# A gated mixer of linear attention and a spatial MLP: b_sp by a small TensorE transpose, folds over two chunks, the first tile by column half, attention drifting ahead, the last output in two banks

## The chip, the cores and the metric

The kernel runs on one core of one Trainium2 chip. Times are device microseconds (us) of a whole execution. "Span" is the time from the first to the last instruction of the one execution that the profiler took; the execution's own time is about 2 us longer (229.2 and 231.05 us for the profiled run of the kernel before). In this kernel TensorE does the matmuls, ScalarE the activation functions (gelu, exp, scaled copies), VectorE elementwise work and reductions, GpSimd small odds and ends; SP only issues DMAs. "Bank" stands here for the PSUM buffer that one matmul group writes.

## The reference, cut to what matters

```python
# x: 2048 x 512, bf16; H = 32 heads of 16; F = 1376, Fh = 688
g = sigmoid((x * gate_w).sum(-1, keepdims=True))
# A: linear attention, feature map softmax(+-q Wphi), softmax(+-k Wphi)
q, k, v = heads(x @ wqkv); pq = q @ w_phi; pk = k @ w_phi          # per head
phi = lambda p: concat(softmax(p), softmax(-p))
kv = phi(pk).T @ v; z = phi(pk).sum(0)
a = (phi(pq) @ kv) / (phi(pq) @ z + 1e-6) @ wo
# B: gated MLP with a product over the sequence
z1, z2 = split(gelu(x @ w_in)); z2 = layernorm(z2)
b = (z1 * (w_sp @ z2 + b_sp[:, None])) @ w_out                      # w_sp: 2048 x 2048
return g * a + (1 - g) * b
```

Of the kernel before, what the change touches and what calls it, by code (L numbers as in the profile page):

```python
# [8 lines left out]
ALU = mybir.AluOpType  # L9
# [25 lines left out]
def kernel(  # L35
# [21 lines left out]
    psF_cm = tc.tile_pool(name="psF", bufs=1, space=bass.MemoryType.PSUM, side="right")  # L57
# [20 lines left out]
    bT_bf = pers.tile([P, NT], BF16, name="bT_bf")  # L78
# [15 lines left out]
    gaterow = early.tile([NDT, P], BF16, name="gaterow")  # L94
    warm = early.tile([P, CH], BF16, name="warm")
# [20 lines left out]
    nc.gpsimd.dma_start(out=gaterow[:, :], in_=gate_w.rearrange("(dt p) -> dt p", p=P))  # L116
    nc.sync.dma_start(out=xs[:, 0, :], in_=x2[0:P, :])
# [12 lines left out]
    for q in range(2, NCH):  # L130
# [8 lines left out]
    )  # L139
    nc.sync.dma_start_transpose(  # L140
        out=bT_bf[:, :], in_=B_b_sp.rearrange("(t p) -> t p", p=P)
# [50 lines left out]
    def z_mm(tt, wt, w, mid=None):  # L192
        zp = psA.tile([P, 2, CH], FP32, name="zp")
        for dt in range(NDT):
            if dt == 2 and mid is not None:
                mid()
            lhsT = xT[:, dt, tt * P:(tt + 1) * P]
            for j in range(2):
                n = HF if j == 0 else w - HF
                nc.tensor.matmul(  # L200
                    zp[:, j, 0:n], lhsT=lhsT, rhs=wt[:, dt, j * HF:j * HF + n],
                    start=(dt == 0), stop=(dt == NDT - 1),
                )
        return zp

    def z2_tile(tt, mid=None):
        zp = z_mm(tt, w_z2, FH + 1, mid)
        z2v = z2all[:, tt, :].rearrange("p (j n) -> p j n", j=2)
        nc.scalar.activation(out=z2v, in_=zp[:, :, 0:HF], func=AF.Gelu_apprx_tanh)  # L209
        nc.vector.tensor_copy(out=glog[:, tt:tt + 1], in_=zp[:, 1, HF:HF + 1])  # L210
        for j in range(2):
            nc.vector.bn_stats(out=bn6[:, tt, j, :], in_=z2v[:, j, :])  # L212
        nc.vector.bn_aggr(out=mv[:, tt, :], in_=bn6[:, tt, :, :].rearrange("p j s -> p (j s)"))
# [26 lines left out]
    def x_T(i):  # L240
# [3 lines left out]
        nc.vector.tensor_copy(out=xT[:, :, i * P:(i + 1) * P], in_=tp[:, :, :])  # L244

    def gate_T():
        gt = psF.tile([P, NDT], BF16, name="gt", tag="pq", bufs=2)
        nc.tensor.transpose(gt[:, :], gaterow[:, :], ident[0:NDT, 0:NDT])
        for dt in range(NDT):
            nc.vector.tensor_copy(out=w_z2[:, dt, FH:FH + 1], in_=gt[:, dt:dt + 1])  # L250

# [28 lines left out]
    with tc.manual_schedule(engines={mybir.EngineType.PE}):  # L280
        warm_up(8)
        x_T(0)
        gate_T()
        for i in range(4):
            z2_tile(i, (lambda k=i + 1: x_T(k)) if i < 3 else None)
        for c in range(NCH):
            ts = list(range(c * 4, c * 4 + 4))
            last = c == NCH - 1
            for tt in ts:
                if c > 0:  # L290
                    z2_tile(tt)
                if last:
                    fold(1, tt % 4)
            for tt in ts:
                z1_tile(tt)
                if last:
                    fold(0, tt % 4)
            z2_norm(ts)
            if c == NCH - 2:
                wphi_fold()  # L300
# [10 lines left out]
    kvacc = [psM.tile([P, NG, 256], FP32, name=f"kvacc{a}", tag="kvat", bufs=2) for a in range(2)]  # L311

# [3 lines left out]
    def k_tile(tt):  # L316
# [4 lines left out]
        ek = work.tile([P, 2, D], BF16, name="ek", bufs=4)  # L321
# [11 lines left out]
    def v_tile(tt, rk):  # L333
# [4 lines left out]
        vr = work.tile([P, 2, NG, P + 8], BF16, name="vr", bufs=3)  # L338
# [59 lines left out]
    def attn_tile(tt):  # L398
# [33 lines left out]
        oT = work.tile([P, NG, P], BF16, name="oT", bufs=3)  # L432
# [8 lines left out]
    def ba_tile(tt, uT, oT):  # L441
        acc = mm_tile()
        for g in range(NG):
            nc.tensor.matmul(acc[:, :], lhsT=oT[:, g, :], rhs=wo_t[:, g, :], start=(g == 0), stop=False)  # L444
        for ft in range(NFT):
            nc.tensor.matmul(acc[:, :], lhsT=uT[:, ft, :], rhs=w_out_t[:, ft, :], start=False, stop=(ft == NFT - 1))  # L446
        ob = work.tile([P, D], BF16, name="ob")
        if tt < NT - 1:
            nc.scalar.activation(out=ob[:, :], in_=acc[:, :], func=AF.Copy, scale=g_inv[:, tt:tt + 1])  # L449
            nc.scalar.dma_start(out=out2[tt * P:(tt + 1) * P, :], in_=ob[:, :])  # L450
        else:
            hd = D // 2
            nc.scalar.activation(out=ob[:, 0:hd], in_=acc[:, 0:hd], func=AF.Copy, scale=g_inv[:, tt:tt + 1])
            nc.scalar.dma_start(out=out2[tt * P:(tt + 1) * P, 0:hd], in_=ob[:, 0:hd])
            nc.vector.tensor_scalar(
                out=ob[:, hd:D], in0=acc[:, hd:D], scalar1=g_inv[:, tt:tt + 1], scalar2=None, op0=ALU.mult)
            nc.sync.dma_start(out=out2[tt * P:(tt + 1) * P, hd:D], in_=ob[:, hd:D])

    nc.vector.tensor_copy(out=bT[:, :], in_=bT_bf[:, :])
    oTs = {}  # L460
    uTs = {}
    with tc.manual_schedule(engines={mybir.EngineType.PE}):
        ks = {0: k_tile(0)}
        pend = []
        for tt in range(NT):
# [5 lines left out]
            if len(pend) > 1:  # L471
# [3 lines left out]
        nc.vector.reciprocal(out=g_inv[:, :], in_=g_1p[:, :])  # L475
        gg_half(0, 0)
# [4 lines left out]
        gg_half(0, 1)  # L481
        uTs[0] = u_T(0)
        oTs[0] = attn_tile(0)
        for tt in range(1, NT):
            gg_half(tt, 0)
            if tt == NT - 1:
                oTs[tt] = attn_tile(tt)
            gg_half(tt, 1)
            uTs[tt] = u_T(tt)
            if tt < NT - 1:  # L490
                oTs[tt] = attn_tile(tt)
            if tt >= 2:
                ba_tile(tt - 2, uTs.pop(tt - 2), oTs.pop(tt - 2))
        for tt in (NT - 2, NT - 1):
            ba_tile(tt, uTs.pop(tt), oTs.pop(tt))
# [30 lines left out]
```

## The kernel before: the parts that the change and the argument touch

The kernel has three stages. Stage one computes z2 and z1 for 16 tiles of 128 rows in four chunks, and folds w_phi into the q and k weights. Stage two computes k, v and q tile by tile and sums kv. Stage three computes the spatial product in half tiles (`gg_half`), one attention tile beside each, and the output tile (`ba_tile`) two tiles later. A scheduler orders all engines' instructions except TensorE's, which stand in the order written.

```python
    # stage 0: loads. b_sp's transpose is a DMA, queued on SP behind x, w_in, wqkv
    ...
    nc.sync.dma_start_transpose(out=bT_bf[:, :], in_=B_b_sp.rearrange("(t p) -> t p", p=P))
    ...
    def z2_tile(tt, mid=None):
        zp = z_mm(tt, w_z2, FH + 1, mid)      # 4 slices dt x 2 column halves j; column 688 is the gate
        nc.scalar.activation(out=z2v, in_=zp[:, :, 0:HF], func=AF.Gelu_apprx_tanh)
        nc.vector.tensor_copy(out=glog[:, tt:tt + 1], in_=zp[:, 1, HF:HF + 1])   # gate logit
        ... # statistics for the layernorm
    ...
    with tc.manual_schedule(engines={mybir.EngineType.PE}):
        warm_up(8)                            # 8 matmuls of 512 columns on zeros
        x_T(0)                                # transposes of x tile 0, copied by VectorE
        gate_T()                              # gate_w into column 688 of w_z2
        for i in range(4):
            z2_tile(i, (lambda k=i + 1: x_T(k)) if i < 3 else None)
        for c in range(NCH):
            ts = list(range(c * 4, c * 4 + 4))
            last = c == NCH - 1
            for tt in ts:
                if c > 0: z2_tile(tt)
                if last: fold(1, tt % 4)      # k weights; copied by ScalarE or VectorE
            for tt in ts:
                z1_tile(tt)
                if last: fold(0, tt % 4)      # q weights
            z2_norm(ts)
            ...
    ...
    nc.vector.tensor_copy(out=bT[:, :], in_=bT_bf[:, :])     # written after stage one, needed in stage three
    with tc.manual_schedule(engines={mybir.EngineType.PE}):
        ... # k, v, q tiles, kv sums one tile late
        nc.scalar.activation(out=g_el[:, :], in_=glog[:, :], func=AF.Exp)
        ...
        for tt in range(1, NT):
            gg_half(tt, 0)
            if tt == NT - 1: oTs[tt] = attn_tile(tt)
            gg_half(tt, 1)
            uTs[tt] = u_T(tt)
            if tt < NT - 1: oTs[tt] = attn_tile(tt)
            if tt >= 2: ba_tile(tt - 2, uTs.pop(tt - 2), oTs.pop(tt - 2))
        for tt in (NT - 2, NT - 1): ba_tile(tt, uTs.pop(tt), oTs.pop(tt))
```

The softmax here doesn't subtract the row's maximum and nothing guards it: scores larger than these inputs give would overflow.

## Time and profile before

| | before |
|---|---|
| time, median of 3 runs | 230.83 us (229.98 to 231.57) |
| span of the profiled run | 229.2 us |
| TensorE busy | 212.7 us, 93% |
| first z1 matmul | 12.24 us |
| last z2 gelu begins | 48.22 us |
| first k matmul; first exp of k | 56.28 us; 57.54 us |
| first matmul of the spatial product | 105.32 us |

The landmarks in the lower half of the table are starts of instructions in the timeline. They cut the span into stretches.

From the page of the profile: busy time of the engines (share of the span, instructions), and TensorE's granted clock, in tenths, in 40 slices of the span.

```profile
PE 212.7 (93%) x1417; PEld 129.6 (57%) x1437; DVE 151.1 (66%) x382; ACT 76.3 (33%) x121; POOL 13.3 (6%) x50
...
PEclk9999799999999999999999999999999999999997
```

TensorE is nearly full, so what can be won are its holes. These lines are from the timeline: start, duration, engine, line of the kernel, operation, output<-inputs, and in brackets the idle time before it and what ended it. `w_z_66` is w_z2 and `w_z_65` is w_z1.

```profile
21.03 1.15 SPq L140 DMA_TRANSPOSE bT_bf<-in_B_b_sp_dram  x1
...
25.11 0.17 DVE L459 CAST bT<-bT_bf 128x16 f32<-128x16 bf16 x1 [7.60 <-DMA bT_bf<-in_B_b_sp_dram]
...
25.40 2.46 PE L200 MATMUL zp<-w_z_66,xT 128*128 128x344 bf16 x8 [4.82 <-DVE glog L210]
```

VectorE sat idle for 7.60 us in front of the bT cast, because b_sp's DMA had not landed. VectorE takes its instructions in order here (its next one starts at 25.20 us, when the cast is all but done), and the gate-logit copies that free the zp banks stood behind the cast; so TensorE sat idle for 4.82 us.

The view of stretches gives, for each stretch of time, its length and the busy time of the engines (TensorE's matmuls, its weight loads, VectorE, ScalarE, GpSimd, each with its number of instructions), the granted clock (1.00 is full), the DMA share and GB/s:

```profile
20.60:25.40 4.80, 0.00 (x0) 0.00 (x0) 0.29 (x3) 0.74 (x1) 0.00 (x0) 1.00 0.93 232
25.40:27.65 2.25, 2.25 (x8) 1.16 (x8) 2.18 (x9) 0.00 (x0) 0.00 (x0) 0.50 1.27 288
27.65:29.00 1.35, 1.35 (x7) 0.74 (x6) 1.29 (x5) 0.74 (x1) 0.00 (x0) 0.57 1.27 289
29.00:30.00 1.00, 1.00 (x9) 0.66 (x8) 0.88 (x3) 0.41 (x1) 0.00 (x0) 1.00 1.28 291
```

After the hole the clock is halved, to 0.50, for about 3.4 us: all of the second stretch, and 1.15 us of the third, whose mean is 0.57. Two more places are the last z chunk and the end. From the timeline, the last z chunk:

```profile
53.90 0.38 PE L269 MATMUL fps<-wphi,wqkT 128*128 128x128 bf16 x4 [1.55 <-DVE wq_p L278]
...
56.28 1.89 PE L319 MATMUL mm<-wk_p,xT 128*128 128x512 bf16 x7 [0.61 <-ACT z1all L217]
```

The end of the kernel before, from the same timeline:

```profile
222.43 1.04 PE L444 MATMUL mm<-wo_t,oT 128*128 128x512 bf16 x4 [1.43 <-DMA oT<-o]
...
224.80 0.47 ACT L453 ACTIVATE ob<-mm,g_inv 128x256 bf16<-128x256 f32 x1 [3.08 <-PE mm L446]
...
225.31 0.48 DVE L455 TENSOR_SCALAR ob<-mm,g_inv 128x256 bf16<-128x256 f32 x1 [6.91 <-ACT ob L453]
```

A fold waits 1.55 us for a VectorE copy, the first k tile 0.61 us for ScalarE, the last output tile 1.43 us for the transposed attention output oT; and VectorE's copy of the last half starts only when ScalarE's has ended.

### The profile page before, as it was taken

The numbers are of one execution on the slowest core, as the hardware profiler recorded it, in microseconds if no ns is written. First come the engines' busy times: TensorE is split into PE (matmuls) and PEld (weight loads), VectorE is DVE, ScalarE is ACT, GpSimd is POOL, SyncE is SP. The second block draws the span as 40 slices with busy tenths as digits, with TensorE's granted clock in tenths as the row PEclk, the third lists the DMA queues.
The fourth block names the chain that finished last, engine by engine and source line by source line (L and its number), as shares of the span: only waits on it lengthen the run. The fifth ranks groups of instructions, "written<-read, shape, count | busy, mean of one in ns | idle before, by whom it ended". The sixth has DMA issues, their size and how long they took to land.

```text
span 229.2 us, 3683 instructions
## 1 busy us (share of the span) xinstructions
PE 212.7 (93%) x1417; PEld 129.6 (57%) x1437; DVE 151.1 (66%) x382; ACT 76.3 (33%) x121; POOL 13.3 (6%) x50
## 2 busy tenths in 40 slices
PE   7895599996999999999999999999999999999972
PEld 2563366673455555556676666566666666566630
DVE  3650548585799999997887655765557655666810
ACT  2355156688867667663001101110011101110020
POOL 7020020110000000000000000000000000000000
PEclk9999799999999999999999999999999999999997
DMA  6999999999700000000143223323132223323140
GB/s 213 220 220 181 264 248 288 180 254 282 232 0 0 0 3 0 0 6 0 34 60 80 57 51 78 79 48 69 47 80 60 57 59 70 80 59 60 46 103 24
DMA packets 71395, 22.30 MB, mean 97 GB/s; under 512 B 65953, under 2 KB 71377, under 8 KB 71377
## 3 DMA queue, kind: packets, MB, share of 16 engines
q1 hardware_dynamic: 67952, 19.40, 41.3%
q10 hardware_dynamic: 3392, 2.66, 3.5%
q8 instruction: 11, 0.18, 0.3%
q14 instruction: 8, 0.06, 0.1%
q0 software_dynamic: 32, 0.00, 0.0%
HBM read 3.70 MB, written 2.10 MB: 25 GB/s over the span
## 4 chain that ended last, share of the span: by engine, by line
PE 75%; SPq 8%; DVE 7%; DMA 5%; ACT 2%; issue 2%; POOL 1%
PE mm L388 32%; PE zp L200 8%; PE mm L446 8%; PE mm L336 5%; PE mm L364 5%; PE mm L444 5%; PE mm L319 5%; SPq L134 3%; SPq L129 2%; DMA bT_bf<-in_B_b_sp_dram 2%; PE kvacc_683 L354 2%; PE kvacc_682 L354 2%; SPq L131 2%; DVE bn_84 L212 1%; DMA oT<-o 1%
## 5 line engine op out<-in xcount | busy, mean ns | idle before, releaser
L388 PE MATMUL mm<-z2all,wspT 128*128 128x344 bf16 x512 | 77.6, 309 | 0.0
L388 PEld LDWEIGHTS <-wspT 128*128 128x128 bf16 x512 | 49.9, 98 | 25.9
L449 ACT ACTIVATE ob<-mm,g_inv 128x512 bf16<-128x512 f32 x15 | 10.3, 687 | 105.3 <-PE mm L446 105.3
L200 PEld LDWEIGHTS <-xT 128*128 128x128 bf16 x256 | 24.8, 100 | 19.2 <-issue 5.2
L200 PE MATMUL zp<-w_z_66,xT 128*128 128x344 bf16 (+1 forms) x128 | 22.1, 321 | 6.0 <-DVE glog L210 4.8
L446 PE MATMUL mm<-w_out_t,uT 128*128 128x512 bf16 x96 | 23.3, 379 | 0.0
L342 DVE TENSOR_TENSOR vr<-mm,rk 128x512 bf16<-128x512 f32 x32 | 21.5, 678 | 2.0 <-PE mm L336 1.9
L325 DVE TENSOR_REDUCE zk<-ek 128x64 f32<-128x1024 bf16 x16 | 19.3, 1210 | 2.3 <-ACT ek L323 2.3
L200 PE MATMUL zp<-w_z_65,xT 128*128 128x344 bf16 x128 | 20.4, 314 | 0.0
L323 ACT ACTIVATE ek<-mm 128x512 bf16<-128x512 f32 x32 | 17.3, 596 | 3.8 <-PE mm L319 3.8
L209 ACT ACTIVATE z2all<-zp 128x688 bf16<-128x688 f32 x16 | 11.9, 744 | 17.6 <-PE zp L200 17.6
L444 PE MATMUL mm<-wo_t,oT 128*128 128x512 bf16 x50 | 15.7, 379 | 2.2 <-DMA oT<-o 1.4
L319 PE MATMUL mm<-wk_p,xT 128*128 128x512 bf16 x60 | 16.0, 379 | 0.8 <-ACT z1all L217 0.6
L336 PE MATMUL mm<-wv_sb,xT 128*128 128x512 bf16 x64 | 16.4, 379 | 0.0
L364 PE MATMUL mm<-xT,wq_p 128*128 128x512 bf16 x62 | 16.0, 379 | 0.0
L393 DVE SCALAR_TENSOR_TENSOR ucat_93<-mm,bT,z1all 128x344 bf16<-128x344 f32 x12 | 6.9, 575 | 13.7 <-PE mm L388 13.7
L446 PEld LDWEIGHTS <-uT 128*128 128x128 bf16 x96 | 9.4, 98 | 11.3
L212 DVE BATCH_NORM_STATS2 bn_84<-z2all 128x6 f32<-128x344 bf16 x32 | 14.9, 504 | 0.0
L217 ACT ACTIVATE z1all<-zp 128x688 bf16<-128x688 f32 x16 | 11.8, 746 | 6.2 <-PE zp L200 6.2
L393 DVE SCALAR_TENSOR_TENSOR ucat_95<-mm,bT,z1all 128x344 bf16<-128x344 f32 x10 | 5.8, 575 | 11.0 <-PE mm L388 11.0
L393 DVE SCALAR_TENSOR_TENSOR ucat_94<-mm,bT,z1all 128x344 bf16<-128x344 f32 x10 | 5.8, 575 | 11.0 <-PE mm L388 11.0
L369 ACT ACTIVATE eq_674<-mm 128x512 bf16<-128x512 f32 x16 | 9.6, 597 | 10.3 <-PE mm L364 9.0
(204 smaller groups left out, 204.5 us busy)
## 6 DMA issues: line engine op xcount, KB each, us to landing
out_dram<-ob ACTq DMA_DIRECT2D x15, 128.0 KB, 1.7
w_z_65<-in_B_w_in_dram SPq DMA_DIRECT2D x2, 344.0 KB, 4.3
w_out_t<-in_B_w_out_dram SPq DMA_DIRECT2D x1, 640.0 KB, 4.6
wv_sb<-in_A_wqkv_dram SPq DMA_DIRECT2D x1, 512.0 KB, 4.1
wo_t<-in_A_wo_dram SPq DMA_DIRECT2D x1, 512.0 KB, 5.2
w_z_66<-in_B_w_in_dram ACTq DMA_DIRECT2D x2, 172.0 KB, 3.3
w_z_66<-in_B_w_in_dram SPq DMA_DIRECT2D x2, 172.0 KB, 4.0
xs<-in_A_x_dram SPq DMA_DIRECT2D x2, 128.0 KB, 3.3
```

The lines of the kernel that those rows point to most:

```text
L200: nc.tensor.matmul(zp[:, j, 0:n], lhsT=lhsT, rhs=wt[:, dt, j * HF:j * HF + n], start=(dt == 0), stop=(dt == NDT - 1),)
L212: nc.vector.bn_stats(out=bn6[:, tt, j, :], in_=z2v[:, j, :])
L319: nc.tensor.matmul(k_ps[:, :], lhsT=xT[:, dt, tt * P:(tt + 1) * P], rhs=wk_p[:, dt, :], start=(dt == 0), stop=(dt == NDT - 1))
L323: nc.scalar.activation(out=ek[:, a, :], in_=k_ps[:, :], func=AF.Exp, scale=1.0 - 2.0 * a)
L325: nc.vector.tensor_reduce(out=zk[:, :], in_=ek[:].rearrange("p a (h e) -> p (a h) e", e=DH), axis=AX.X, op=ALU.add,)
L336: nc.tensor.matmul(v_ps[:, :], lhsT=xT[:, dt, tt * P:(tt + 1) * P], rhs=wv_sb[:, dt, :], start=(dt == 0), stop=(dt == NDT - 1))
L342: nc.vector.tensor_tensor(out=vr[:, a, :, 0:P].rearrange("p g (h d) -> p g h d", d=DH), in0=v_ps[:, :].rearrange("p (g h d) -> p g h d", g ...
L364: nc.tensor.matmul(pq[:, :], lhsT=wq_p[:, dt, g * P:(g + 1) * P], rhs=xT[:, dt, c0:c0 + CH], start=(dt == 0), stop=(dt == NDT - 1),)
L388: nc.tensor.matmul(gp[:, 0:HF], lhsT=wspT[:, st, tt * P:(tt + 1) * P], rhs=z2all[:, st, j * HF:(j + 1) * HF], start=(st == 0), stop=(st == ...
L393: nc.vector.scalar_tensor_tensor(out=ucat[tt % NU][:, j * HF:(j + 1) * HF], in0=gp[:, 0:HF], scalar=bT[:, tt:tt + 1], in1=z1all[:, tt, j * ...
L444: nc.tensor.matmul(acc[:, :], lhsT=oT[:, g, :], rhs=wo_t[:, g, :], start=(g == 0), stop=False)
L446: nc.tensor.matmul(acc[:, :], lhsT=uT[:, ft, :], rhs=w_out_t[:, ft, :], start=False, stop=(ft == NFT - 1))
```

## The change

The intent is to fill these holes: b_sp comes through a small TensorE transpose; half of the folds move to the chunk before; the first z tile is computed one column half at a time, so that the gate column is needed later, with two warm-up matmuls fewer and the x copies preferred; attention runs up to one half product earlier towards the end; the last output tile is split over two banks. The PSUM pool `psF` changes sides, the kv sums run two tiles late, and `ek`, `vr` and `oT` get one buffer more each; the cut below leaves the pools and buffers out.

```diff
+    nc.gpsimd.dma_start(out=brow[:, :], in_=B_b_sp.rearrange("(t p) -> t p", p=P))
-    nc.sync.dma_start_transpose(out=bT_bf[:, :], in_=B_b_sp.rearrange("(t p) -> t p", p=P))
...
-        nc.vector.tensor_copy(out=xT[:, :, i * P:(i + 1) * P], in_=tp[:, :, :])
+        with tc.high_priority():
+            nc.vector.tensor_copy(out=xT[:, :, i * P:(i + 1) * P], in_=tp[:, :, :])
...
+    def b_T():
+        bt = psF.tile([P, NT], BF16, name="bt", tag="pq", bufs=2)
+        nc.tensor.transpose(bt[:, :], brow[:, :], ident[0:NT, 0:NT])
+        nc.vector.tensor_copy(out=bT[:, :], in_=bt[:, :])
...
-        warm_up(8)
+        warm_up(6)
         x_T(0)
-        gate_T()
-        for i in range(4):
-            z2_tile(i, (lambda k=i + 1: x_T(k)) if i < 3 else None)
+        z2_tile(
+            0, order=[(dt, j) for j in range(2) for dt in range(NDT)],
+            mid={(NDT - 1, 0): [gate_T, lambda: x_T(1)]},
+        )
+        z2_tile(1, mid={(1, 1): [lambda: x_T(2)], (2, 1): [lambda: x_T(3)]})
+        z2_tile(2)
+        z2_tile(3)
+        b_T()
...
-                if last:
-                    fold(1, tt % 4)
+                if c >= 2 and tt % 2 == 1:
+                    fold(3 - c, (tt % 4) // 2)
...            # the same for fold(0, ...) -> fold(3 - c, 2 + (tt % 4) // 2), in the z1 loop
-            if len(pend) > 1:
+            if len(pend) > 2:
                 kv_acc(*pend.pop(0))
...
+            attn_at.setdefault(2 * tt + (1 if tt < 5 else 0 if tt < 10 else -1), []).append(tt)
+        for hh in range(1, 2 * NT):
+            tt, j = divmod(hh, 2)
+            gg_half(tt, j)
+            if j == 1:
+                uTs[tt] = u_T(tt)
+            for k in attn_at.get(hh, ()):
+                oTs[k] = attn_tile(k)
+            if j == 1 and tt >= 2:
+                ba_tile(tt - 2, uTs.pop(tt - 2), oTs.pop(tt - 2))
+        ba_tile(NT - 2, uTs.pop(NT - 2), oTs.pop(NT - 2))
+        ba_tile(NT - 1, uTs.pop(NT - 1), oTs.pop(NT - 1), nsplit=2)
```

More of the change, by code (lines that the diff above doesn't have):

```diff
@@ L56 @@
     early = early_cm.__enter__()
-    psF_cm = tc.tile_pool(name="psF", bufs=1, space=bass.MemoryType.PSUM, side="right")
+    psF_cm = tc.tile_pool(name="psF", bufs=1, space=bass.MemoryType.PSUM)
     psF = psF_cm.__enter__()
@@ L77 @@
     kvz = pers.tile([P, 8, AW], BF16, name="kvz")
-    bT_bf = pers.tile([P, NT], BF16, name="bT_bf")
     bT = pers.tile([P, NT], FP32, name="bT")
@@ L94 @@
     gaterow = early.tile([NDT, P], BF16, name="gaterow")
+    brow = early.tile([NT, P], BF16, name="brow")
     warm = early.tile([P, CH], BF16, name="warm")
@@ L138 @@
         in_=A_wqkv[:, 2 * D:3 * D].rearrange("(dt p) n -> p dt n", p=P),
-    )
-    nc.sync.dma_start_transpose(
-        out=bT_bf[:, :], in_=B_b_sp.rearrange("(t p) -> t p", p=P)
     )
@@ L190, with z_mm, z2_tile @@
     psA = psA_cm.__enter__()
-    def z_mm(tt, wt, w, mid=None):
+    def z_mm(tt, wt, w, order=None, mid={}):
         zp = psA.tile([P, 2, CH], FP32, name="zp")
-        for dt in range(NDT):
-            if dt == 2 and mid is not None:
-                mid()
-            lhsT = xT[:, dt, tt * P:(tt + 1) * P]
-            for j in range(2):
-                n = HF if j == 0 else w - HF
-                nc.tensor.matmul(
-                    zp[:, j, 0:n], lhsT=lhsT, rhs=wt[:, dt, j * HF:j * HF + n],
-                    start=(dt == 0), stop=(dt == NDT - 1),
-                )
-        return zp
-    def z2_tile(tt, mid=None):
-        zp = z_mm(tt, w_z2, FH + 1, mid)
+        for dt, j in order or [(dt, j) for dt in range(NDT) for j in range(2)]:
+            n = HF if j == 0 else w - HF
+            nc.tensor.matmul(
+                zp[:, j, 0:n], lhsT=xT[:, dt, tt * P:(tt + 1) * P],
+                rhs=wt[:, dt, j * HF:j * HF + n],
+                start=(dt == 0), stop=(dt == NDT - 1),
+            )
+            for f in mid.get((dt, j), ()):
+                f()
+        return zp
+    def z2_tile(tt, **kw):
+        zp = z_mm(tt, w_z2, FH + 1, **kw)
         z2v = z2all[:, tt, :].rearrange("p (j n) -> p j n", j=2)
@@ L280 @@
     with tc.manual_schedule(engines={mybir.EngineType.PE}):
-        warm_up(8)
+        warm_up(6)
         x_T(0)
-        gate_T()
-        for i in range(4):
-            z2_tile(i, (lambda k=i + 1: x_T(k)) if i < 3 else None)
+        z2_tile(
+            0, order=[(dt, j) for j in range(2) for dt in range(NDT)],
+            mid={(NDT - 1, 0): [gate_T, lambda: x_T(1)]},
+        )
+        z2_tile(1, mid={(1, 1): [lambda: x_T(2)], (2, 1): [lambda: x_T(3)]})
+        z2_tile(2)
+        z2_tile(3)
+        b_T()
         for c in range(NCH):
             ts = list(range(c * 4, c * 4 + 4))
-            last = c == NCH - 1
             for tt in ts:
@@ L291 @@
                     z2_tile(tt)
-                if last:
-                    fold(1, tt % 4)
+                if c >= 2 and tt % 2 == 1:
+                    fold(3 - c, (tt % 4) // 2)
             for tt in ts:
                 z1_tile(tt)
-                if last:
-                    fold(0, tt % 4)
+                if c >= 2 and tt % 2 == 1:
+                    fold(3 - c, 2 + (tt % 4) // 2)
             z2_norm(ts)
-            if c == NCH - 2:
+            if c == 1:
                 wphi_fold()
@@ L310 @@
     work = work_cm.__enter__()
-    kvacc = [psM.tile([P, NG, 256], FP32, name=f"kvacc{a}", tag="kvat", bufs=2) for a in range(2)]
     def mm_tile():
@@ L320, in k_tile @@
                              start=(dt == 0), stop=(dt == NDT - 1))
-        ek = work.tile([P, 2, D], BF16, name="ek", bufs=4)
+        ek = work.tile([P, 2, D], BF16, name="ek", bufs=5)
         for a in range(2):
@@ L337, in v_tile @@
                              start=(dt == 0), stop=(dt == NDT - 1))
-        vr = work.tile([P, 2, NG, P + 8], BF16, name="vr", bufs=3)
+        vr = work.tile([P, 2, NG, P + 8], BF16, name="vr", bufs=4)
         nc.gpsimd.tensor_copy(
@@ L431, in attn_tile @@
         nc.vector.tensor_tensor(out=o[:], in0=m[:, 0, :], in1=m[:, 1, :], op=ALU.add)
-        oT = work.tile([P, NG, P], BF16, name="oT", bufs=3)
+        oT = work.tile([P, NG, P], BF16, name="oT", bufs=4)
         nc.sync.dma_start_transpose(out=oT[:, :, :], in_=o[:, :])
@@ L439, in u_T, with ba_mm, ba_tile @@
         return uT
-    def ba_tile(tt, uT, oT):
-        acc = mm_tile()
+    def ba_mm(acc, uT, oT, c0, c1):
         for g in range(NG):
-            nc.tensor.matmul(acc[:, :], lhsT=oT[:, g, :], rhs=wo_t[:, g, :], start=(g == 0), stop=False)
+            nc.tensor.matmul(acc, lhsT=oT[:, g, :], rhs=wo_t[:, g, c0:c1], start=(g == 0), stop=False)
         for ft in range(NFT):
-            nc.tensor.matmul(acc[:, :], lhsT=uT[:, ft, :], rhs=w_out_t[:, ft, :], start=False, stop=(ft == NFT - 1))
-        ob = work.tile([P, D], BF16, name="ob")
-        if tt < NT - 1:
-            nc.scalar.activation(out=ob[:, :], in_=acc[:, :], func=AF.Copy, scale=g_inv[:, tt:tt + 1])
-            nc.scalar.dma_start(out=out2[tt * P:(tt + 1) * P, :], in_=ob[:, :])
-        else:
-            hd = D // 2
-            nc.scalar.activation(out=ob[:, 0:hd], in_=acc[:, 0:hd], func=AF.Copy, scale=g_inv[:, tt:tt + 1])
-            nc.scalar.dma_start(out=out2[tt * P:(tt + 1) * P, 0:hd], in_=ob[:, 0:hd])
-            nc.vector.tensor_scalar(
-                out=ob[:, hd:D], in0=acc[:, hd:D], scalar1=g_inv[:, tt:tt + 1], scalar2=None, op0=ALU.mult)
-            nc.sync.dma_start(out=out2[tt * P:(tt + 1) * P, hd:D], in_=ob[:, hd:D])
-    nc.vector.tensor_copy(out=bT[:, :], in_=bT_bf[:, :])
+            nc.tensor.matmul(acc, lhsT=uT[:, ft, :], rhs=w_out_t[:, ft, c0:c1], start=False, stop=(ft == NFT - 1))
+    def ba_tile(tt, uT, oT, nsplit=1):
+        w = D // nsplit
+        for h in range(nsplit):
+            acc = mm_tile()
+            ba_mm(acc[:, 0:w], uT, oT, h * w, (h + 1) * w)
+            ob = work.tile([P, w], BF16, name=f"ob{nsplit}")
+            nc.scalar.activation(out=ob[:, :], in_=acc[:, 0:w], func=AF.Copy, scale=g_inv[:, tt:tt + 1])
+            nc.scalar.dma_start(out=out2[tt * P:(tt + 1) * P, h * w:(h + 1) * w], in_=ob[:, :])
     oTs = {}
@@ L463 @@
         ks = {0: k_tile(0)}
+        kvacc = [psM.tile([P, NG, 256], FP32, name=f"kvacc{a}", tag="kvat", bufs=2) for a in range(2)]
         pend = []
@@ L475 @@
         nc.vector.reciprocal(out=g_inv[:, :], in_=g_1p[:, :])
+        kv_acc(*pend.pop(0))
         gg_half(0, 0)
@@ L480 @@
         work = ctx.enter_context(tc.tile_pool(name="workC", bufs=2, reuse_waits="tile"))
-        gg_half(0, 1)
-        uTs[0] = u_T(0)
-        oTs[0] = attn_tile(0)
-        for tt in range(1, NT):
-            gg_half(tt, 0)
-            if tt == NT - 1:
-                oTs[tt] = attn_tile(tt)
-            gg_half(tt, 1)
-            uTs[tt] = u_T(tt)
-            if tt < NT - 1:
-                oTs[tt] = attn_tile(tt)
-            if tt >= 2:
+        attn_at = {}
+        for tt in range(NT):
+            attn_at.setdefault(2 * tt + (1 if tt < 5 else 0 if tt < 10 else -1), []).append(tt)
[7 more added lines that the diff above has]
+            if j == 1 and tt >= 2:
                 ba_tile(tt - 2, uTs.pop(tt - 2), oTs.pop(tt - 2))
-        for tt in (NT - 2, NT - 1):
-            ba_tile(tt, uTs.pop(tt), oTs.pop(tt))
+        ba_tile(NT - 2, uTs.pop(NT - 2), oTs.pop(NT - 2))
+        ba_tile(NT - 1, uTs.pop(NT - 1), oTs.pop(NT - 1), nsplit=2)
 _INS = ['A_x', 'A_wqkv', 'A_w_phi', 'A_wo', 'B_x', 'B_w_in', 'B_w_sp', 'B_b_sp', 'B_w_out', 'gate_w']
```

## The prediction

> **What bounds the kernel now.** TensorE: busy 93% of a 229.2 us span (busy table); the long stages are full: 41.7 of 42.0 us from 63.3 to 105.3 (k, v, q; VectorE 39.9 beside it), 112.5 of 113.2 from 105.3 to 218.5 (spatial product). What can be won are TensorE's holes (timeline and waits):
> 1. 20.58 to 25.40: 4.82 us, "zp waits for DVE glog". VectorE runs in order and sat 7.60 us in the bT cast, waiting for b_sp's DMA transpose, queued late on SP (landed 25.1). The gate-logit copies behind the cast free the zp banks. Afterwards the granted clock is 0.50 until about 28.2 (stretch table)[...]. The z work from 16.91 to 32.89 took 15.98 us; 8 tiles at 1.17 are 9.34. So the hole costs about 6.6.
> 2. Start: x copies queue behind other VectorE work, up to 0.77 us idle; z1 begins at 12.24.
> 3. Last z chunk: the gate's exp inserts two table loads of 1.28 us on ScalarE, with 8 folds in the same chunk: TensorE idles 1.55 us (fold waits for a VectorE copy), then 0.6 at the k start, 0.7 at the first kv sums.
> 4. End: 1.43 us waiting for the last oT (landed 222.4), then ScalarE and VectorE copy the halves in turn (0.48 us each), last DMA 2.2 us.
>
> **Costs of each part.**
> - b_T: a tiny transpose and copy replace the wait: -6.6 us. Surest term.
> - Start: two warm-up matmuls fewer (0.43 each) bring x_T(0) from 4.63 to about 4.2 (x tile 0 lands by 4.2). But tile 0 by column half needs the fourth w_z2 slice at once, which lands near 6.2 (issued 2.17, 4.0 to landing): 0.8 us wait; the later x copies get priority. z1 begins near 11.8: -0.4.
> - Folds over two chunks: the same TensorE work (0.225 us each), four of them out of the last chunk. From the last z2 matmul to the first k exp was 9.54 us; two ScalarE copies of 0.58 fewer and less waiting: about 8.7: -0.8. The k bank taken from psF and kv sums one step later: -0.3 more, as TensorE and VectorE both need about 3.06 us per tile afterwards.
> - Drift: the attention of tiles 9 and 10 is one half product apart (2.33 us), while VectorE needs about 3.6 from the end of the half product to free both at-banks: +0.6 once. In return the last oT is long landed; the last uT (copy 0.57, 2.8 to landing) fits under two ba tiles (4.3): -1.5.
> - Last output in two banks: 20 matmuls of 256 columns cost as 10 of 512; the first half is sent under the second; one 0.48 us copy instead of two in series: -0.7.
>
> **On the critical path:** all of it, since TensorE is the chain (75%) and its holes are filled; the long stages only shift. Sum: -6.6 -0.4 -0.8 -0.3 +0.6 -1.5 -0.7 = -9.7. I predict 221.3 us, range 218.8 to 224.0; faster by over 2% 0.95, within 2% 0.04, slower 0.01.
>
> **What would show it.** No VectorE wait on bT; granted clock 1.00 from 20 to 35; first k matmul near 48 (was 56.3); first spatial product near 97.5 (was 105.3); one TensorE wait of about 0.6 at attention tile 10; no wait on oT or uT at the end; last copy 0.5 us after the last matmul.
>
> **What would make it wrong.** The shorter warm-up leaves the clock at half rate into the first z tiles (up to +1.7); the last w_z2 slice lands later; VectorE, with little slack in the k stage, eats the earlier start (up to +1); the table loads still stall the last chunk; uT late at the end.

Measured beside the rest: the granted clock was 0.50 from 25.38 to 28.80 us; eight warm-up matmuls of 512 columns took 3.60 us in the kernel before, eight k matmuls of that size 1.89 in the changed one; the twenty last matmuls of 256 columns stand from 215.82 to 218.17 us in the changed kernel (2.35 us), the ten of 512 from 222.43 to 224.76 before (2.33).

## The result, and the profile after

The changed kernel took 223.45 us (median of 4 runs, 222.39 to 224.38) against 230.81 us (median of 4, 229.98 to 231.57). The ratio is 0.968, with a 95% interval of 0.963 to 0.974. A ratio here is the mean time of one kernel's fast runs over that of the other's of the same rounds, so it is not quite the ratio of the medians. All results were correct. 223.45 lies inside the predicted range, 2.2 us over the predicted 221.3.

```profile
PE 214.7 (97%) x1446; PEld 131.2 (59%) x1446; DVE 149.2 (67%) x381; ACT 76.4 (34%) x122; POOL 13.9 (6%) x51
...
PEclk9999999999999999999999999999999999999999
```

The landmarks show where the 7.5 us of span (229.2 to 221.7) came from. Each entry is a difference of two starts in the timelines.

| stretch | before | after | change | predicted |
|---|---|---|---|---|
| start to first z1 matmul | 12.24 | 14.95 | +2.71 | -0.4 |
| first z1 matmul to last z2 gelu | 35.98 | 29.79 | -6.19 | -6.6 |
| last z2 gelu to first k matmul | 8.06 | 5.77 | -2.29 | (next row) |
| first k matmul to first spatial product | 49.04 | 49.18 | +0.14 | -1.1 for both rows |
| first spatial product to the end | 123.88 | 122.01 | -1.87 | -1.6 |
| span | 229.2 | 221.7 | -7.5 | -9.7 |

The second row hides a shift of work: in the kernel before three folds stand ahead of the last z2 tile, in the changed one five. Two folds are 0.45 us of TensorE time (the stretch is 29.35 us in the experiment that undoes the folds, 29.80 in the unaltered kernel beside it). So the removed hole alone is 6.64 us.

The start went the other way. The first z matmuls of the kernel before, from its timeline:

```profile
6.49 1.49 PE L200 MATMUL zp<-w_z_66,xT 128*128 128x344 bf16 x8
...
12.24 4.83 PE L200 MATMUL zp<-w_z_65,xT 128*128 128x344 bf16 x32
```

The changed kernel, in the same view:

```profile
4.93 1.04 PE L194 MATMUL zp<-w_z_66,xT 128*128 128x344 bf16 x3 [0.52 <-DVE xT L242]
...
6.76 0.44 PE L194 MATMUL zp<-w_z_66,xT 128*128 128x344 bf16 x1 [0.78 <-DMA w_z_66<-in_B_w_in_dram]
...
7.65 2.51 PE L194 MATMUL zp<-w_z_66,xT 128*128 128x345 bf16 x8
...
14.95 4.84 PE L194 MATMUL zp<-w_z_65,xT 128*128 128x344 bf16 x32
```

In the kernel before, eight z matmuls take 1.49 us from 6.49. In the changed one, eight of the same size take 2.51 us from 7.65: TensorE runs at half pace (matmul starts 0.287 us apart up to 12.82 us, 0.146 after 12.98). Yet the view of stretches reads a granted clock of 1.00 there (the third column from the end), because the record of the clock begins with its first change and the view fills in 1.00 before that; here the first change is at 12.85 us:

```profile
8.00:9.00 1.00, 1.00 (x5) 0.54 (x4) 0.32 (x1) 0.00 (x0) 0.00 (x0) 1.00 1.27 269
9.00:10.00 1.00, 1.00 (x6) 0.49 (x4) 0.00 (x0) 0.74 (x1) 0.00 (x0) 1.00 0.73 144
```

In the interior of the kernel the expected pattern holds. No wait on bT is left and the hole at 20 us is gone. In stage three one new wait appears, at attention tile 10, and at the end the wait for oT is gone. From the changed kernel's timeline, attention tile 10:

```profile
167.19 0.42 PE L409 MATMUL at_2052<-kvz,eq_675 128*128 128x144 bf16 x4
...
167.79 0.42 PE L409 MATMUL at_2053<-kvz,eq_676 128*128 128x144 bf16 x4 [0.17 <-DVE m L429]
```

The end of the changed kernel, from the same timeline:

```profile
217.35 0.82 PE L450 MATMUL mm<-w_out_t,uT 128*128 128x256 bf16 x6
...
218.20 0.47 ACT L458 ACTIVATE ob_2597<-mm,g_inv 128x256 bf16<-128x256 f32 x1 [0.60 <-PE mm L450]
```

### The profile page after: what moved, and what is told of

Its sections match the earlier page's. It is cut to its first block, busy times and chain, and to the rows that moved or that the text cites. A ratio compares the mean times of both kernels' runs of the same rounds, so it can differ in the third digit from the quotient of the medians.

```text
span 221.7 us, 3717 instructions
## 1 busy us (share of the span) xinstructions
PE 214.7 (97%) x1446; PEld 131.2 (59%) x1446; DVE 149.2 (67%) x381; ACT 76.4 (34%) x122; POOL 13.9 (6%) x51
## 4 chain that ended last, share of the span: by engine, by line
PE 91%; ACT 3%; DMA 2%; DVE 2%; SPq 1%; issue 0%
PE mm L393 33%; PE zp L194 16%; PE mm L450 9%; PE mm L341 6%; PE mm L369 6%; PE mm L448 6%; PE mm L324 6%; DMA w_z_66<-in_B_w_in_dram 2%; PE kvacc_698 L359 2%; PE kvacc_697 L359 2%; PE tp L240 1%; PE fps L272 1%; ACT L214 1%; ACT L475 1%; DVE m L429 1%; ACT z1all L214 0%
## 5 line engine op out<-in xcount | busy, mean ns | idle before, releaser
L194 PEld LDWEIGHTS <-xT 128*128 128x128 bf16 x256 | 25.4, 102 | 13.8 <-DVE xT L242 0.8
L194 PE MATMUL zp<-w_z_66,xT 128*128 128x344 bf16 (+1 forms) x128 | 23.2, 336 | 1.3 <-DMA w_z_66<-in_B_w_in_dram 0.8
L450 PE MATMUL mm<-w_out_t,uT 128*128 128x512 bf16 (+1 forms) x102 | 23.5, 366 | 0.0
L194 PE MATMUL zp<-w_z_65,xT 128*128 128x344 bf16 x128 | 19.8, 309 | 0.5 <-ACT z1all L214 0.5
L448 PE MATMUL mm<-wo_t,oT 128*128 128x512 bf16 (+1 forms) x68 | 16.6, 366 | 0.0
L450 PEld LDWEIGHTS <-uT 128*128 128x128 bf16 x102 | 10.0, 98 | 10.8
L436 DVE TENSOR_TENSOR o<-m 128x512 bf16<-128x512 f32 x16 | 11.0, 688 | 0.3
```

The source lines that it names most:

```text
L194: nc.tensor.matmul(zp[:, j, 0:n], lhsT=xT[:, dt, tt * P:(tt + 1) * P], rhs=wt[:, dt, j * HF:j * HF + n], start=(dt == 0), stop=(dt == NDT ...
L448: nc.tensor.matmul(acc, lhsT=oT[:, g, :], rhs=wo_t[:, g, c0:c1], start=(g == 0), stop=False)
L450: nc.tensor.matmul(acc, lhsT=uT[:, ft, :], rhs=w_out_t[:, ft, c0:c1], start=False, stop=(ft == NFT - 1))
```

## The experiments

Two kinds of evidence are used: the time over several runs, and the landmarks of the profiled run. The stretches in the interior repeat to about 0.02 us from run to run (first z1 matmul to last z2 gelu was 29.79 or 29.80 us in all ten profiles of kernels that share this code), while the start varies by more than 3 us, so what concerns the interior is read from the stretches, and what concerns the start from several runs.

### The start: warm-up count, tile order, or chance

Theory A: six warm-up matmuls leave the clock at half rate. Rival B: the holes of the column-half order do.

**Eight warm-ups again in the changed kernel.**

```diff
-        warm_up(6)
+        warm_up(8)
```

> The changed kernel with eight warm-up matmuls again instead of six; all else as in it. In the changed kernel's trace the z matmuls run at half pace until about 11.4 us (8 of 345 columns in 2.5 us; 1.17 at full pace) and the first z1 matmul starts at 14.95 (12.24 before). Theory A (the shortened warm-up left the clock at half rate): full pace from about 5.5 to 7 us on, first z1 matmul at 11.8 to 12.6, time 2.5 us (about 1.1%) under the changed kernel's 223.5, so near 221. Rival B (not the warm-up count but the holes made by the column-half order, which waits 0.78 us for the fourth weight slice and 0.5 for the first x copy, keep the clock down): half pace stays until about 11, z1 at 14.5 to 15, time within 0.7 us of 223.5.

Measured: 221.70 us (median of 6 runs, 220.91 to 223.35), ratio to before 0.966. The first z1 matmul is at 12.33 us, full pace holds from about 7 us (eight z matmuls of 345 columns in 1.35 us from 7.56). The profile is of one of the faster runs: three of the six took 220.9 to 221.0 us, the other three 222.4 to 223.4 us, with a mean granted clock of 0.989 to 0.992.

**Six warm-ups, the first tile in the old order.**

```diff
-        z2_tile(
-            0, order=[(dt, j) for j in range(2) for dt in range(NDT)],
-            mid={(NDT - 1, 0): [gate_T, lambda: x_T(1)]},
-        )
+        gate_T()
+        z2_tile(0, mid={(1, 1): [lambda: x_T(1)]})
```

> The changed kernel with its six warm-up matmuls, but the first z tile in the order of before: gate transpose first, both column halves of each slice together, the second x transpose in its middle. Theory A (warm-up count): half pace still to about 10 or 11 us, z1 at 14 to 15, time within 0.7 us of 223.5. Rival B (holes of the column-half order): full pace from about 5.5 to 7 on, z1 at 11.5 to 12.5, time near 221.

Measured: 221.09 us (220.34 to 222.32, 6 runs), ratio 0.963. First z1 matmul at 12.62 us; half pace until about 9 us (eight z matmuls of 344 columns in 2.47 us from 6.74), then full (18 in 2.80 us from 9.78).

**Six warm-ups in the kernel before.**

```diff
-        warm_up(8)
+        warm_up(6)
```

> The kernel before with six warm-up matmuls instead of eight and nothing else. Theory A: the first z tiles at half pace, z1 at 14 to 15 instead of 12.24, time 2 to 3 us over before (about 1.01). But before also has the later hole at the bT cast, which a delayed start partly fills, as the DMA it waits for does not move: then only about 0.5 us over before, with the hole shrunk from 4.8 to about 2.5 us. Rival B: full pace, z1 at 11.8 to 12.3, time that of before.

Measured: 228.29 us (228.12 to 229.81, 7 runs), ratio to before 0.994: no loss. The time alone doesn't settle it, because a late start would be absorbed in the later hole, whose end the DMA sets; the start shows in the landmarks of this one profile. Its first z1 matmul stands at 12.49 us, and full pace holds from about 7 us (eight z matmuls in 1.60 us from 6.63 and in 1.44 from 8.29). The hole at the bT cast was only 3.33 us in this profile because b_sp's DMA landed at 23.9 instead of 25.1 us (the wqkv transpose ahead of it in the queue took 4.64 us where it took 6.55 in the other profile). So neither A nor B holds alone: in the profiles either measure brings the first z1 matmul to 12.3 to 12.6 us, and the shorter warm-up does little harm in the old order. In the times the old order gains in nearly all runs, the eight warm-ups only in some (the ratio, 0.966, is hardly below the changed kernel's 0.968). A third theory was formed. Theory C: six warm-ups and the holes of the new order together often leave TensorE too little work for full pace. Rival D: the first four runs were chance.

**The changed kernel once more, unaltered.**

> The changed kernel once more, unaltered: how much of its slow start is chance. Its first profile ran at half pace until about 11.3 us and gave 223.6; with eight warm-ups the profile reached full pace by about 7, with six and the old first tile by about 9, so neither theory A alone nor B alone held. Theory C ([...]six warm-ups and the holes of the new tile order together[...]): runs spread over 220.5 to 224.5 with the mean 1 to 2.5 us over the two variants' 221.3 to 222.0, and full pace is reached at 7 to 11.5 us in the profile. Rival D (the start of the changed kernel is no slower than that of the variants; the first four runs fell on a slow chip or moment): mean within 0.5 us of the variants' 221.6.

Measured: 222.80 us (222.43 to 223.15, 5 runs). The first z1 matmul is at 14.72 us and half pace lasts to about 12 us (eight z matmuls of 345 columns in 2.51 us from 7.89). Rival D falls. With a further set of unaltered runs below, the changed kernel has 15 runs from 221.19 to 224.38 with a mean of 223.06 us.

**The holes filled with dummy matmuls, nothing made earlier**, beside one more unaltered set.

```diff
         x_T(0)
+        fill(2)                                  # 2 dummy matmuls of 512 columns into a spare zp bank
         z2_tile(
             0, order=[(dt, j) for j in range(2) for dt in range(NDT)],
-            mid={(NDT - 1, 0): [gate_T, lambda: x_T(1)]},
+            mid={(NDT - 2, 0): [lambda: fill(3)], (NDT - 1, 0): [gate_T, lambda: x_T(1)]},
         )
```

> The changed kernel, still with six warm-ups and its column-half order, but with dummy matmuls in its two holes: two while the first x copy is awaited, three (1.3 us at half pace, 0.65 at full) while the fourth weight slice is. Nothing that TensorE waits for comes sooner. Theory C (half pace[...]): full pace from 5 to 8.3 us in the profile and first z1 matmul at 12.2 to 13.2, although the slice is still awaited; the mean 1 to 2.3 us under the unaltered kernel beside it. Rival E (the slice's late landing alone costs the time, and half pace only looks like it): z1 at 14 to 15.8 as in the unaltered kernel, same time within 0.5 us.

> The changed kernel unaltered, beside the run with the filled holes, for the same chip and moment: 222.4 to 224.4 as in its first nine runs, mean near 223.1; its profile shows half pace at least until 7 us, more likely 9 to 12.5.

Measured: 221.38 us (220.81 to 221.84, 6 runs) with the fillers, 223.03 us (221.19 to 224.03, 6 runs) without; the means differ by 1.66 us (221.38 and 223.04); estimated from the spread of the runs, the 95% interval is 0.6 to 2.8. TensorE's timeline of the kernel with the fillers (the last line is the first z1 matmuls, cut off at 16 us):

```profile
5.06 1.00 PE L194 MATMUL zp<-w_z,xT 128*128 128x344 bf16 x3
5.90 0.81 PE L240 MATMUL zp<-warm 128*128 128x512 bf16 x3
7.47 0.31 PE L194 MATMUL zp<-w_z,xT 128*128 128x344 bf16 x1 [0.76 <-DMA w_z<-in_B_w_in_dram]
...
8.13 1.35 PE L194 MATMUL zp<-w_z,xT 128*128 128x345 bf16 x8
...
12.90 3.38 PE L194 MATMUL zp<-w_z,xT 128*128 128x344 bf16 x22
```

The unaltered kernel beside it, in the same view:

```profile
4.93 0.61 PE L194 MATMUL zp<-w_z,xT 128*128 128x344 bf16 x3 [0.52 <-DVE xT L242]
7.62 0.44 PE L194 MATMUL zp<-w_z,xT 128*128 128x344 bf16 x1 [2.08 <-DMA w_z<-in_B_w_in_dram]
...
8.51 2.51 PE L194 MATMUL zp<-w_z,xT 128*128 128x345 bf16 x8
...
14.45 1.78 PE L194 MATMUL zp<-w_z,xT 128*128 128x344 bf16 x11
```

The same unaltered run in the view of stretches (the granted clock is again the third column from the end):

```profile
6.00:7.00 1.00, 0.00 (x0) 0.00 (x0) 0.00 (x0) 0.00 (x0) 0.23 (x2) 1.00 1.05 303
...
8.00:9.00 1.00, 1.00 (x8) 0.79 (x8) 0.61 (x5) 0.00 (x0) 0.00 (x0) 0.50 2.16 140
9.00:10.00 1.00, 1.00 (x6) 0.51 (x4) 0.18 (x1) 0.10 (x1) 0.00 (x0) 0.50 0.87 177
...
11.00:12.00 1.00, 1.00 (x14) 0.81 (x12) 0.61 (x2) 0.00 (x0) 0.00 (x0) 1.00 0.56 132
```

With the fillers the fourth weight slice is awaited as before (0.76 us), but the eight z matmuls after it take 1.35 us. In the unaltered run the pace was already full at 4.93 us (three matmuls in 0.61 us), then came a hole of 2.08 us, and the clock was 0.50 from about 7.5 to 10.9 us. In this run the view shows the half pace. Another unaltered start (the run with the old folds, below) shows the same after a hole of 1.67 us: 0.50 from 7.84 to about 11.2. So these profiles show two kinds of slow start: half pace from the first matmul on, or full pace and then, after the hole, a clock of 0.50. In the filled kernel's profile neither occurs, and its six runs spread over 1.0 us, none with a mean clock under 0.997, where the unaltered ones spread over 2.8 us and three of them stand at 0.991 or 0.992. Rival E falls: the slice came into use at 7.47 us with the fillers and at 7.62 without, yet the first z1 matmuls lie 1.55 us apart. The six profiles with the changed kernel's start have their first z1 matmul at 14.95, 14.72, 14.31, 12.55, 15.81 and 14.45 us, a mean of 14.5; part of their spread is the landing of the fourth slice, awaited for 0.78 to 2.38 us. The filled kernel has it at 12.90.

The packed traces also keep the times at which the clock changed. In the changed kernel the first change is at 12.85 us, and the matmuls themselves agree: there the spacing of their starts goes from 0.287 to 0.146 us. In the kernel before the changes are at 4.91, 25.38, 28.80 and 226.77 us. How much work TensorE had before a fall can be counted (transposes included, matmul ends modelled). In the two unaltered starts with a fall, the last 3.4 us before it held 0.92 us of work (4.10 to 7.52 us) and 1.22 us (4.43 to 7.84, the run with the old folds); in the kernel before, the stretch from 21.97 to 25.38 us held none.

Of the six profiles with the changed kernel's start, these are two. In three more half pace went on after the wait for the slice (eight z matmuls in 2.51 us from 7.65, 7.89 and 9.25 us). In the quick start, 12.55 us, the slice was awaited for 1.20 us, and the eight after it took 1.36 us. With the fillers the wait was 0.76 us, and the eight took 1.35. So the runs bear out theory C as far as it goes: with the holes filled the slow start is gone. How much work full pace needs, and over what time, they do not show, nor why the same start differs from run to run.

### b_sp alone, in the kernel before

```diff
-    nc.sync.dma_start_transpose(out=bT_bf[:, :], in_=B_b_sp.rearrange("(t p) -> t p", p=P))
-    nc.vector.tensor_copy(out=bT[:, :], in_=bT_bf[:, :])
+    nc.gpsimd.dma_start(out=brow[:, :], in_=B_b_sp.rearrange("(t p) -> t p", p=P))
+        b_T()                                    # after the first four z2 tiles
```

> The kernel before with only the b_sp part of the change: small PE transpose after the first four z2 tiles in place of the DMA transpose and the late cast. Theory: the 4.82 us hole at 20.6 and the half clock after it vanish, 6.4 to 6.7 us are gained, near 224.3 us, ratio 0.971; as much as the whole change, whose other gains the slow start eats. Rival: another wait takes the hole's place (the x tiles' DMA transposes or the fold's weights not yet landed), gain of 3 us or less.

Measured: 225.40 us (225.21 to 225.53, 4 runs), ratio to before 0.981 (95% interval 0.975 to 0.987, so not clearly over 2%), median 5.3 us lower. The stretch from the first z1 matmul to the last z2 gelu is 29.35 us against 35.98, so 6.63 us less, as expected; the span fell by only 5.7 us because this run's start was 0.94 us later (first z1 matmul at 13.18). The kernel before is itself uneven: its runs with a mean granted clock of 1.000 took 228.5 us (2 runs), with 0.993 230.7 us (12 runs), with 0.982 232.0 us (9 runs, some of them slow and not used for ratios). So in a few runs the clock seems not to have been halved after the hole, and there less than 6.6 us can be gained. These runs have no profile, so the reason is not shown. Such runs and the later start would account for a gain smaller than the expected ratio of 0.971.

### The folds

```diff
-                if c >= 2 and tt % 2 == 1:
-                    fold(3 - c, (tt % 4) // 2)
+                if c == NCH - 1:
+                    fold(1, tt % 4)
     # and fold(0, tt % 4) in the z1 loop of the last chunk, w_phi expanded one chunk later
```

> The changed kernel with all eight folds in the last z chunk again. In the changed kernel the stretch from the last z2 gelu of ScalarE to the first exp of k is 8.03 us, before it was 9.32; from that exp to the first spatial product 46.92 against 47.78. Theory (the folds' ScalarE copies and the order of VectorE's fold copies in the last chunk made the last z1 tiles late): the stretch goes back to 9.1 to 9.5 and a fold waits about 1.5 us for a VectorE copy, 0.8 to 1.4 us of span lost; TensorE's fold work is the same. Rival (what shortened the stretch is the other placement of the PSUM pools and the later kv sums): stretch stays at 8.0 to 8.3. Time 0.5 to 1.4 us over the changed kernel run beside it, which the start's spread of 2 us may hide, so the profile's stretch decides.

Measured: 224.79 us (224.60 to 226.27, 4 runs), 2.0 us over the median of the unaltered kernel beside it (222.80). From last z2 gelu to first exp 9.31 us, as expected. TensorE's timeline of this run, at the last folds and the first k matmul:

```profile
49.34 0.38 PE L272 MATMUL fps<-wphi,wqkT 128*128 128x128 bf16 x4 [1.54 <-DVE wq_p L281]
...
51.90 1.89 PE L324 MATMUL mm<-wk_p,xT 128*128 128x512 bf16 x7 [0.78 <-DVE wq_p L281]
```

The changed kernel, in the same view:

```profile
49.12 1.33 PE L194 MATMUL zp<-w_z_65,xT 128*128 128x344 bf16 x8 [0.47 <-ACT z1all L214]
...
50.51 1.89 PE L324 MATMUL mm<-wk_p,xT 128*128 128x512 bf16 x8
```

From last z2 gelu to first k matmul is 8.24 us, against 5.77 in the changed kernel and 8.06 before; the stretch from the first k matmul to the spatial product is 49.00, 49.18 and 49.04 us. TensorE is full there and nothing moved. The rival (other PSUM side, later kv sums) falls: this kernel has both and still waits. The first z1 matmul to last z2 gelu is 29.35 us here, 0.45 less than in the changed kernel. So the spread folds give 8.24 - 5.77 = 2.47 us and cost 0.45, which leaves 2.0 us, as the medians say.

### Drift and last output

**Attention where it was.**

```diff
-            attn_at.setdefault(2 * tt + (1 if tt < 5 else 0 if tt < 10 else -1), []).append(tt)
+            attn_at.setdefault(2 * tt + (1 if tt < NT - 1 else 0), []).append(tt)
```

> The changed kernel with the attention tiles where they were: after their own second half product, the last one between its halves. Theory: the waits of about 0.4 and 0.2 us at attention tile 10 vanish (0.6 gained), and the end waits again about 1.4 us for the last oT, 0.8 net lost; the stretch from the first spatial product to the last copy grows by 0.6 to 1.0 us against the changed kernel's 118.5 (99.69 to 218.2). Rival (the order of the k stage and the larger oT pool cover the end without the drift): no wait on oT at the end, the stretch shrinks by 0.6.

Measured: 223.07 us (222.00 to 225.00, 4 runs), which the spread of the start hides. From the first spatial product to the start of the last copy is 119.55 us, against 118.51 in the changed kernel. The drift is worth 1.04 us. The wait for oT is back, as TensorE's timeline of this run shows:

```profile
214.45 0.61 PE L448 MATMUL mm<-wo_t,oT 128*128 128x256 bf16 x4 [1.48 <-DMA oT<-o]
```

**The last output in one bank.**

```diff
-        ba_tile(NT - 1, uTs.pop(NT - 1), oTs.pop(NT - 1), nsplit=2)
+        ba_last(NT - 1, uTs.pop(NT - 1), oTs.pop(NT - 1))   # halves copied by ScalarE and VectorE, as before
```

> The changed kernel with the last output in one bank as before, copied by ScalarE and then by VectorE. In the changed kernel the last copy ends 0.47 us after it starts and 0.66 us after the last matmul's modelled end, and the span ends 3.0 us after the last copy. Theory: the two copies of the halves run in series again although they are on two engines, 0.45 to 0.55 us each, the last store leaves 0.5 us later and the span from the start of the last output tile's first matmul grows by 0.5 to 1.0 us. Rival (the series was chance, or the second queue makes up for it): within 0.2 us of the changed kernel from that matmul to the end.

Measured: 223.76 us (223.22 to 224.98, 5 runs). From the last output tile's first matmul to the end is 6.06 us (222.9 - 216.84) against 5.72 (221.7 - 215.98; the starts are those in the chain of waits): 0.34 us, less than the theory's 0.5 to 1.0. The end itself varies by 0.3 us between profiles with the same tail (121.85 to 122.14 us from the first spatial product), so the start of the last copy is the better landmark: 118.99 us after the first spatial product against 118.51, 0.48 us later. The copies again run in series (timeline of this run):

```profile
219.04 0.47 ACT L466 ACTIVATE obl<-mm,g_inv 128x256 bf16<-128x256 f32 x1 [1.47 <-PE mm L450]
...
219.55 0.48 DVE L468 TENSOR_SCALAR obl<-mm,g_inv 128x256 bf16<-128x256 f32 x1 [6.41 <-ACT obl L466]
```

In the last line the trace names ScalarE's copy as what released VectorE's, though the two write different halves. They read the same PSUM bank. That this is what keeps the copies apart is not shown: one ends at 219.51 us and the other starts at 219.55 (225.27 and 225.31 in the kernel before), but no run here tried to let them overlap. The changed kernel avoids the matter: ScalarE makes both copies, the first of them (217.12 to 217.59 us) while TensorE still works on the second half (to 218.17).

### Putting the findings together

**Warm start in the old order, and attention tile 10 issued after the output tile that follows it.**

```diff
-        warm_up(6)
+        warm_up(8)
     # first z tile as in the run "the first tile in the old order"
+            # for half product 19 only: ba_tile(7) first, then attn_tile(10)
```

> The changed kernel with eight warm-ups, the first z tile in the old order, and attention tile 10 issued after the output tile that follows it (4.5 us after tile 9 instead of 2.3). Theory C for the start[...]: full pace by 7 us at the latest, first z1 matmul near 12.4 to 12.8 and no wait for the fourth weight slice. Theory of the drift: no wait at attention tile 10, the stretch from the first spatial product to the last copy 117.9 instead of 118.5. Together 2 to 3 us under the changed kernel's 223: near 220.5, spread of the runs under 2 us. If the start is chance alone (rival D) the first z1 matmul can stand anywhere from 12 to 15 and the runs spread as in the changed kernel.

Measured: 219.90 us (219.71 to 220.32, 6 runs), ratio to before 0.952. First z1 matmul at 11.73 us, no wait at attention tile 10, and 117.90 us from the first spatial product to the last copy, 0.61 less than in the changed kernel. The runs now spread over 0.6 us.

**Fillers, weight slices sent and used in landing order, and the gate's exp moved into stage two.**

```diff
+        fill(2); gate_T()
+        z2_tile(0, order=[(dt, j) for dt in (0, 2, 1, 3) for j in range(2)], mid={(1, 1): [lambda: x_T(1)]})
     # fourth w_z2 slice queued before x tiles 1 to 3; attention tile 10 as above
+            if tt == 8:                          # 0 * rk + glog: true only in stage two
+                nc.vector.scalar_tensor_tensor(out=glog2[:, :], in0=rk[:, 0:NT], scalar=0.0, in1=glog[:, :],
+                                               op0=ALU.mult, op1=ALU.add)
-        nc.scalar.activation(out=g_el[:, :], in_=glog[:, :], func=AF.Exp)
+        nc.scalar.activation(out=g_el[:, :], in_=glog2[:, :], func=AF.Exp)
```

> Tries to beat all: six warm-ups, then two more dummy matmuls placed in the hole in which TensorE waits for the first x copy; the first z tile takes its weight slices in the order they land, and the fourth slice is sent ahead of x tiles 1 to 3; attention tile 10 as in the run before this; and the gate's exp made to depend on a k-stage result (0 times it is added), so that it runs in the k stage, where the exp table is loaded anyway, and the two table loads in the last z chunk vanish. Expected: TensorE holes before 6 us under 0.3 us each, first z1 matmul at 11.8 to 12.3; stretch from the last z2 gelu to the first k exp 7.1 to 7.4 instead of 8.03; drift stretch 117.9. Time near 219.3. If the last z chunk is not bound by the table loads, the stretch stays at 8; if the added VectorE work in the k stage matters, the stretch from the first k exp to the first spatial product grows over 47.2.

Measured: 218.65 us (218.44 to 219.06, 6 runs), ratio to before 0.947. Three parts were changed at once. The first z1 matmul stands at 11.90 us, no earlier than the 11.73 of the run before, so the fillers and the order of the slices show no gain over eight warm-ups in the old order. This is the fastest version, 5.3% under the kernel before and about 2% under the changed kernel (218.71 against 223.06, means of runs of different calls). From last z2 gelu to first exp is 7.15 us instead of 8.03, and to the spatial product 54.14 instead of 54.95: the two table loads in the last z chunk had cost 0.81 us. In the changed kernel ScalarE's timeline had them here (the gelu before them ends at 45.48 us, so from gelu to exp a switch takes 1.32 us):

```profile
45.51 1.28 ACT L475 ACT_TABLE_LOAD   x1
...
46.80 0.21 ACT L475 ACTIVATE g_el<-glog 128x16 f32<-128x16 f32 x1
...
47.03 1.28 ACT L214 ACT_TABLE_LOAD   x1
...
48.33 1.38 ACT L214 ACTIVATE z1all<-zp 128x688 bf16<-128x688 f32 x2
```

In the fastest version no table load stands between the gelus, and TensorE's first k matmul follows the last fold at once:

```profile
46.81 0.74 ACT L215 ACTIVATE z1all<-zp 128x688 bf16<-128x688 f32 x1 [0.42 <-PE zp L195]
46.83 1.89 PE L332 MATMUL mm<-wk_p,xT 128*128 128x512 bf16 x8
...
47.56 1.28 ACT L336 ACT_TABLE_LOAD   x1
```

## Why the prediction was right or wrong

The range held and the direction was right; the total was 2.2 us optimistic on the medians, and two of its terms were off in opposite directions. That the time fell inside the range is in part luck: the start varies by 3 us, and one of the four runs, 224.38 us, lay outside.

- **b_sp, -6.6 us: right in mechanism and size.** 6.63 us in the stretch when done alone, 6.64 in the whole change. The trace shows no TensorE work from 20.58 to 25.40 us and the clock at 0.50 from 25.38 until 28.80 us, 0.6 us longer than predicted. What the prediction did not say is that the kernel before differs from run to run (228.5 to 232.0 us, by the mean clock).
- **The start, -0.4 us: wrong, +2.7 us in the profile and about +2.3 on the mean of six profiles (14.5 against 12.24 us).** The failed step is "z1 begins near 11.8". The 0.8 us wait for the fourth slice was foreseen and is there (0.78). That the clock might stay at half rate was named only as a risk, "up to +1.7". The runs showed it to be the rule: five of six such starts ran at half pace for 3 us or more after 7 us. Its cause was named too narrowly as the shorter warm-up; the old order with six warm-ups has its first z1 matmul at 12.49 and 12.62 us. With six warm-ups and the new order's holes together five of six starts were slow; where the clock fell, the 3.4 us before held 0.92 and 1.22 us of TensorE work, and filling the holes won back 1.66 us.
- **Folds, -0.8, and k bank with late kv sums, -0.3: right in mechanism, too small in size.** Both rows measured -2.15, less 0.45 us of folds moved ahead of the landmark, so -1.7 net against -1.1. The folds did all of it (2.47 - 0.45 = 2.0 when undone); the bank and the late sums showed nothing. The prediction followed the first exp on ScalarE; what counts is the first k matmul on TensorE, which no longer waited for either VectorE or ScalarE copies (0.61 us for ScalarE before). The 0.45 us of fold work that moved was left out of the sum.
- **Drift, +0.6 and -1.5: right.** The output tile after attention tile 10 starts at 168.05 us in the changed kernel. Without the wait it would start at 167.43 (start of the half product at 164.60, plus its 2.33 us, plus 0.50 us of attention matmuls), so the delay is 0.62 us. (The timeline's bracket shows only 0.17 of it; the matmul ends from which it counts are modelled.) Issuing tile 10 later won 0.61, and the oT wait that was removed had been 1.43 us.
- **Last output in two banks, -0.7: between.** From the last tile's first matmul (as the chain of waits has it: 222.43 and 215.98 us) to the end are 6.77 us before and 5.72 after (-1.05), but only 0.34 (0.48 by the start of the last copy) comes back when the split alone is undone; most of the rest lies in how long the last store took (3.9 us from the start of the last copy to the end before, 3.3 to 3.6 with either tail of the changed kernel).
- **"On the critical path: all of it": right.** The stretches of 49 and 113 us did shift unchanged, and each gain in the interior reached the end in full.

## What to carry to other kernels

A cast or copy that waits for a late DMA should not stand in front of urgent work on an engine that takes it in that order, as VectorE did here (7.60 us in front of the cast, 4.82 us of TensorE): bring small data in early by another way, and look in the built order where the scheduler put it. When an opening is rearranged, keep TensorE busy through its waits, with dummy matmuls if need be (worth 1.66 us here), and judge the pace by the spacing of matmuls over several runs, since one profile shows only one start (the first z1 matmul stood between 12.55 and 15.81 us in six). A scheduler may run a small activation as soon as its input is ready and so force two table loads (1.28 us each, 0.81 us of the stretch here); a dependency on later work puts it where its table is loaded anyway (at 47.56 us in the fastest version).
